# Attention in front of two Strassen layers on one core: loads three pairs ahead, four score blocks in a row, an immediate bias, tiles moved by 32 bytes

## The chip, the cores and the metric

The kernel runs on one core of one Trainium2 chip. The metric is the device time of one execution in microseconds (us); lower is better. Engines are called as the profile calls them: PE (TensorE, with PEld for its weight loads), DVE (VectorE), ACT (ScalarE), POOL (GpSimd), and SP, whose queue (SPq) issues nearly all DMAs.

## The reference, cut to what matters

```python
scores = scale * np.matmul(q, k.transpose(0, 1, 3, 2)) - np.log(S)   # 4 x 12 heads, S = 448, 64 wide
attn = 1.0 / (1.0 + np.exp(-scores))
out = np.matmul(attn, v)
x = out.transpose(0, 2, 1, 3).reshape(1792, 768)
h = x @ w_in;  x = (h * np.cos(h)) @ w_out                            # 768 -> 2048 -> 768
g = x @ w_gate                                                        # 768 -> 1536
y = (g / (1.0 + np.exp(-g)) * (x @ w_val)) @ w_out2                   # 1536 -> 768
```

Three stages follow each other: attention with a sigmoid in place of a softmax, layer 1 (cosine) and layer 2 (a gated pair). The weights arrive as float64.

## The kernel before

**Attention.** The 48 heads are taken as 24 pairs; two heads lie side by side in partitions 0 to 63 and 64 to 127. For a pair, `load` (L699) brings q and k into a slot of `raw_qk` (L704, two DMAs, three slots, `i % 3`), v into a tile `vs` (L706, three buffers), and the last 64 rows of v into a slot of `last_v` (L708, two small DMAs). `split` (L713) makes a high and a low part of q and k on DVE (tile `qk`, two buffers). `scores` (L720) computes one of four blocks: six matmuls into two of the six score banks, then one sigmoid on ACT (L731) from the banks into a tile `a`; its bias -log(448) is read from a one-column tile `nlog`. `weigh` (L734) multiplies the four blocks by v (L741) and ACT copies the result into the tile `r` (L743). In turn `i` of the pair loop the code issues: the loads of pair i+2, score blocks 0 to 2 of pair i, the split of pair i+1, `weigh(i - 1)`, and score block 3 of pair i. Every engine takes its instructions in the order in which the program lists them.

**Weight conversion.** Float64 weights are turned into float32 on the chip, one tile of 128x768 at a time: a DMA in (tile `lr` or `raw`), one ACT step, five DVE steps (or four and a second one on ACT), a DMA out to a scratch buffer (`swi`, `swo` and so on). Four lent sets of buffers do some of it beside attention (`lend_pool`), and the rest is done during layer 1. A converted tile comes back later into `t`, is summed (`sum`) and split (tiles `wa`, `wb`, `s`) for the matmuls.

**The two layers.** One level of Strassen: 28 units (16 in layer 1, 12 in layer 2) of seven products each (two times seven in layer 2; `seven`, L991, nine matmuls a product) and twelve down steps (`down`, L893, twelve matmuls a step). The moving operand is `x` for the products and `g` for the down steps. The seven combinations of x lie in two tiles: numbers 1, 5, 2 and 6 in `x0`, numbers 7, 3 and 4 in `x1`, which is opened on the other end of the memory when the lent buffers go.

**What sets the order.** An order written by a planner. `Order` simulates each engine with costs from the code; a task names an engine and a time, and the planner issues what can start first. During attention the planner is told by `beside` (L730, called at L767 and L772) how long a pair takes (5.75 us) and how much of each engine attention itself uses. Conversions fill what it believes to be free. So numbers in `beside` move instructions of all later stages too.

**Addresses.** Tiles of a pool lie one behind the other. The tile `small` (8 bytes a partition, 32 taken) stands ahead of `wa`, `s`, and of all that is opened after it on the same side: `qk`, `a`, `vs`, `wb`, `g`. All other sizes are multiples of 64 bytes; so these start 32 bytes behind a multiple of 64. `x0` lies ahead of `small`, on a multiple of 64 (and of 128). `x1` is laid from the other end and starts 96 bytes behind a multiple of 128.

Of the kernel before, what the change touches and what calls it, by code (L numbers as in the profile page):

```python
# [9 lines left out]
F32 = mybir.dt.float32  # L10
# [4 lines left out]
AF = mybir.ActivationFunctionType  # L15
# [135 lines left out]
def block_kernel(  # L151
# [53 lines left out]
    small = xp.tile([P, 2], F32, tag="small", name="small")  # L205
    nlog, warm = small[:, :1], small[:, 1:]
# [30 lines left out]
    LANDING = 5.0  # L237
    ENDS = ((17, 21),)
# [110 lines left out]
    def stashed(n):  # L349
        return False  # L350
# [153 lines left out]
    def operands():  # L504
# [34 lines left out]
        def stash_of(keys):  # L539
            n = keys[0][1] if keys[0][0] == "d" else keys[0][0]  # L540
            layer, h, c = units[n]
            return h, stashed(n), (layer, c) + keys[0][2 if keys[0][0] == "d" else 1:]
# [88 lines left out]
    def beside(time, span, **loads):  # L631

        for engine, load in loads.items():
            order.busy[engine] = max(order.busy.get(engine, 0.0), time) + load
        order.run(time + span)
# [51 lines left out]
    def attention():  # L687
        with tc.tile_pool(name="at", bufs=2) as at:
# [6 lines left out]
            zero = at.tile([P, S], mybir.dt.bfloat16, tag="z", name="z", bufs=1)  # L695
            raw_qk = at.tile([P, 3, 2, S], F32, tag="rqk", name="rqk", bufs=1)
            last_v = at.tile([P, 4, 2, D], F32, tag="lv", name="lv", bufs=1)

            def load(i, q_eng):  # L699

                raw = raw_qk[:, i % 3]
                vs = at.tile([P, NV], F32, tag="vs", name=f"vs{i}", bufs=3)
                for j, half in enumerate(heads):
                    q_eng[j].dma_start(out=raw[half], in_=qk[divmod(i, NP)][:, :, j])  # L704
                there = v[divmod(i, NP)]
                nc.sync.dma_start(out=vs, in_=there[:, :NV])  # L706
# [4 lines left out]
                qkv[i] = (raw, vs.rearrange("p (c j d) -> p c j d", j=2, d=D))  # L711
# [8 lines left out]
            def scores(i, c):  # L720
                both = parts[i]
                a = at.tile([P, 2, S], F32, tag="a", name=f"a{i}_{c}", bufs=8)
# [8 lines left out]
                nc.scalar.activation(out=a, in_=sc, func=AF.Sigmoid, bias=nlog, scale=1.0 / math.sqrt(D))  # L731
                prob[i, c] = a

            def weigh(i):  # L734
                _, vw = qkv.pop(i)
                o = banks[:, 6 + i % 2, :S]
                for c in range(NCH + 1):
                    a = prob.pop((i, c))
                    for j, half in enumerate(heads):
                        value = vw[:, c, j] if c < NCH else last_v[:, i % 4, j]  # L740
                        nc.tensor.matmul(o[half], lhsT=value, rhs=a[:, j], start=c == 0, stop=c == NCH)  # L741
# [14 lines left out]
            stops = []  # L756
            stops.append(lend_pool())
# [21 lines left out]
            time = 5.75 * NPAIR + 6.0  # L779
            beside(time, 3.8, ACT=0.6)  # L780
# [258 lines left out]
    with tc.manual_schedule():  # L1039
        nc.gpsimd.memset(nlog, -math.log(S))  # L1040
# [72 lines left out]
```

## Time and profile before

| | us |
|---|---|
| median of 3 runs (lowest to highest) | 1108.76 (1106.96 to 1112.98) |
| the profiled execution, its own time | 1111.78 |
| its span, first to last instruction | 1110.0 |
| attention, first score matmul to first matmul of layer 1 | 6.33 to 165.18 |
| layers 1 and 2 | 165.18 to 1110.0 |

The span is that of the profiled execution, and 1.78 us of its time lie around it. PE is busy for 97% of the span, but a busy PE need not be at its peak: the time is read from the spacing of its instructions and from the gaps ahead of them.

### The profile page before, as it was taken

The numbers are of one execution on the slowest core, as the hardware profiler recorded it, in microseconds if no ns is written. First come the engines' busy times: TensorE is split into PE (matmuls) and PEld (weight loads), VectorE is DVE, ScalarE is ACT, GpSimd is POOL, SyncE is SP. The second block draws the span as 40 slices with busy tenths as digits, with TensorE's granted clock in tenths as the row PEclk, the third lists the DMA queues.
The fourth block names the chain that finished last, engine by engine and source line by source line (L and its number), as shares of the span: only waits on it lengthen the run. The fifth ranks groups of instructions, "written<-read, shape, count | busy, mean of one in ns | idle before, by whom it ended". The sixth has DMA issues, their size and how long they took to land.

```text
span 1110.0 us, 14774 instructions
## 1 busy us (share of the span) xinstructions
PE 1079.7 (97%) x5507; PEld 931.4 (84%) x5507; DVE 843.9 (76%) x1135; ACT 668.7 (60%) x1001; POOL 130.2 (12%) x104
## 2 busy tenths in 40 slices
PE   7989999999999999999995999999999999999998
PEld 3544558999999899999995999999999999999997
DVE  3878968898899998888999898876459644555644
ACT  5778778777777787777786555544245344333330
POOL 0000000111022110111121200212111200110100
PEclk9999999999999999999998999999999999999999
DMA  8898635544544146455523565542121322112002
GB/s 238 277 249 247 177 110 191 204 168 162 185 149 137 57 149 221 143 179 190 195 91 115 184 225 203 212 142 86 44 71 58 126 88 71 46 55 72 29 1 100
DMA packets 64968, 156.69 MB, mean 141 GB/s; under 512 B 10624, under 2 KB 37248, under 8 KB 64896
## 3 DMA queue, kind: packets, MB, share of 16 engines
q1 hardware_dynamic: 64752, 155.51, 43.4%
q8 instruction: 43, 0.70, 0.3%
q10 hardware_dynamic: 144, 0.23, 0.1%
q14 instruction: 29, 0.24, 0.1%
HBM read 123.47 MB, written 32.24 MB: 140 GB/s over the span
## 4 chain that ended last, share of the span: by engine, by line
PE 83%; DVE 7%; DMA 6%; issue 1%; ACT 1%; SPq 1%; DVEq 0%; ACTq 0%
PE banks L991 43%; PE banks L893 34%; DMA rqk<-in_qk 6%; PE banks L741 3%; PE banks L727 2%; DVE r L229 2%; DVE x L229 1%; DVE u L229 1%; DVE qk L717 1%; DVE u L807 1%; SPq L704 1%; ACT a L731 0%; DVE g L229 0%; DVE qk L716 0%; DVE wa L229 0%
## 5 line engine op out<-in xcount | busy, mean ns | idle before, releaser
L893 PE MATMUL banks<-g,wb 128*128 128x448 f32 x1044 | 229.4, 368 | 0.3 <-DVE g L229 0.2
L991 PE MATMUL banks<-x,wb 128*128 128x448 f32 x1044 | 226.2, 365 | 0.0
L893 PEld LDWEIGHTS banks<-g,wb 128*128 128x128 f32 x1044 | 196.2, 188 | 18.6 <-DVE g L229 0.5
L991 PEld LDWEIGHTS banks<-x,wb 128*128 128x128 f32 x1044 | 196.1, 188 | 15.5 <-ACT banks L226 0.3
L893 PE MATMUL banks<-g,wa 128*128 128x448 f32 x720 | 161.3, 371 | 12.8 <-ACT g L226 11.4
L991 PE MATMUL banks<-x,wa 128*128 128x448 f32 x738 | 161.3, 365 | 0.0
L893 PEld LDWEIGHTS banks<-g,wa 128*128 128x128 f32 x720 | 136.8, 190 | 26.0 <-ACT g L226 11.8
L991 PEld LDWEIGHTS banks<-x,wa 128*128 128x128 f32 x738 | 138.6, 188 | 11.7 <-issue 0.7
L226 ACT ACTIVATE u<-u 128x448 f32<-128x448 f32 x175 | 97.6, 572 | 38.0 <-DVE u L229 27.8
L229 DVE TENSOR_TENSOR u<-u,banks 128x448 f32<-128x448 f32 x120 | 73.9, 617 | 60.8 <-PE banks L991 54.7
L229 DVE TENSOR_TENSOR r<-banks,r 128x896 f32<-128x896 f32 (+1 forms) x69 | 74.2, 1076 | 58.1 <-PE banks L893 57.6
L731 ACT ACTIVATE a<-banks,small 128x896 f32<-128x896 f32 x96 | 89.4, 1010 | 18.3 <-PE banks L727 18.3
L226 ACT ACTIVATE wb<-t 128x768 fp32r<-128x768 f32 x77 | 64.5, 840 | 42.8 <-PE banks L991 33.5
L229 DVE TENSOR_TENSOR wb<-t,wb 128x768 fp32r<-128x768 f32 x77 | 74.2, 967 | 20.5 <-ACT wb L226 20.0
L727 PEld LDWEIGHTS banks<-qk 64*128 64x128 f32 x576 | 50.6, 186 | 41.7 <-ACT a L731 11.4
L727 PE MATMUL banks<-qk 64*128 64x448 f32 x576 | 72.5, 384 | 12.0 <-DVE qk L716 5.7
L991 PE MATMUL banks<-x,s 128*128 128x448 f32 x360 | 80.0, 366 | 0.0
L226 ACT ACTIVATE g<-u 128x448 fp32r<-128x448 f32 x98 | 55.8, 572 | 34.8 <-PE banks L893 17.2
L226 ACT ACTIVATE r<-banks 128x896 f32<-128x896 f32 x52 | 47.8, 919 | 44.8 <-PE banks L893 44.7
L991 PEld LDWEIGHTS banks<-x,s 128*128 128x128 f32 x360 | 67.7, 188 | 5.9
L229 DVE TENSOR_TENSOR g<-u,g 128x448 fp32r<-128x448 f32 x98 | 64.8, 663 | 8.3 <-ACT g L226 8.2
L226 ACT ACTIVATE banks<-banks 128x448 f32<-128x448 f32 x80 | 42.3, 528 | 46.5 <-PE banks L991 45.0
(102 smaller groups left out, 1437.2 us busy)
## 6 DMA issues: line engine op xcount, KB each, us to landing
raw<-in_w_out SPq DMA_DIRECT2D x22, 768.0 KB, 5.5
t<-swi SPq DMA_DIRECT2D x32, 384.0 KB, 3.8
t<-swo SPq DMA_DIRECT2D x64, 192.0 KB, 2.9
rqk<-in_qk SPq DMA_DIRECT2D x47, 224.0 KB, 6.0
raw<-in_w_gate SPq DMA_DIRECT2D x12, 768.0 KB, 4.7
raw<-in_w_val SPq DMA_DIRECT2D x12, 768.0 KB, 4.9
lr<-in_w_in SPq DMA_DIRECT2D x9, 768.0 KB, 8.2
t<-swg SPq DMA_DIRECT2D x17, 384.0 KB, 3.2
```

Of the source, the lines that this page charges most:

```text
L226: return {"ACT": time}, lambda _: nc.scalar.activation(**kw)
L229: return {"DVE": time}, lambda _: nc.vector.tensor_tensor(out=out, in0=in0, in1=in1, op=op)
L704: q_eng[j].dma_start(out=raw[half], in_=qk[divmod(i, NP)][:, :, j])
L717: nc.vector.tensor_tensor(out=both[:, 1], in0=raw, in1=f32(both[:, 0]), op=SUB)
L727: nc.tensor.matmul(sc[:, j], lhsT=both[half, m, 1, starts[c]:starts[c] + P], rhs=both[half, p, 0], start=n == 0, stop=n == 2,)
L731: nc.scalar.activation(out=a, in_=sc, func=AF.Sigmoid, bias=nlog, scale=1.0 / math.sqrt(D))
L741: nc.tensor.matmul(o[half], lhsT=value, rhs=a[:, j], start=c == 0, stop=c == NCH)
L807: yield {"DVE": 0.62}, lambda _: nc.vector.scalar_tensor_tensor(out=u, in0=f, scalar=MAGIC, in1=u, op0=ALU.subtract, op1=ALU.subtract), ti ...
L893: nc.tensor.matmul(banks[:, first + e - d, :N], lhsT=w[:, m, e % KH, :], rhs=g[:, p], start=(i, m, p) == (0, 0, 0) and is_fresh and not pr ...
L991: nc.tensor.matmul(bank, lhsT=w[:, m, k, :], rhs=x[:, k, p, :], start=(k, m, p) == (0, 0, 0) and i in (1, 5), stop=(k, m) == (KH - 1, 1), ...
```

## The change

- The loads of q, k and v are issued three pairs ahead: four slots in `raw_qk`, five buffers of `vs`. `last_v` moves into the third part of `ring`, one slot for each pair of a batch, and is loaded for three pairs with two DMAs (`load_last`).
- The four score blocks of a pair stand in a row, and `weigh(i - 1)` behind them. `a` has seven buffers for eight.
- The bias of the sigmoid is an immediate number; the tile `small` goes, and a tile of 64 bytes (`warm`) takes its place, so that all tiles behind it move from 32 bytes behind a multiple of 64 to a multiple of 64. `x1` does not move. `zero` lies in `sums`.
- The planner's numbers for attention are new: 5.8 us a pair, and a load of each engine with a begin.

```diff
-    small = xp.tile([P, 2], F32, tag="small", name="small")
-    nlog, warm = small[:, :1], small[:, 1:]
+    warm = xp.tile([P, 16], F32, tag="warm", name="warm")
...
-        for engine, load in loads.items():
-            order.busy[engine] = max(order.busy.get(engine, 0.0), time) + load
+        for engine, (begin, load) in loads.items():
+            order.busy[engine] = max(order.busy.get(engine, 0.0), time + begin) + load
         order.run(time + span)
...
-            zero = at.tile([P, S], mybir.dt.bfloat16, tag="z", name="z", bufs=1)
-            raw_qk = at.tile([P, 3, 2, S], F32, tag="rqk", name="rqk", bufs=1)
-            last_v = at.tile([P, 4, 2, D], F32, tag="lv", name="lv", bufs=1)
+            zero = sums.bitcast(mybir.dt.bfloat16)[:, :S]
+            raw_qk = at.tile([P, 4, 2, S], F32, tag="rqk", name="rqk", bufs=1)
+            last_v = ring[:, 2].rearrange("p (s j d) -> p s j d", j=2, d=D)
+            NL = NP // 2
...
-                raw = raw_qk[:, i % 3]
-                vs = at.tile([P, NV], F32, tag="vs", name=f"vs{i}", bufs=3)
+                raw = raw_qk[:, i % 4]
+                vs = at.tile([P, NV], F32, tag="vs", name=f"vs{i}", bufs=5)
...
+            def load_last(i):
+
+                b, k = divmod(i, NP)
                 for j, half in enumerate(heads):
+                    there = v[b][k:k + NL, half, NV + P + j * D:NV + P + (j + 1) * D]
                     nc.sync.dma_start(
-                        out=last_v[heads[1], i % 4, j], in_=there[half, NV + P + j * D:NV + P + (j + 1) * D]
+                        out=last_v[heads[1], i % NP:i % NP + NL, j], in_=there.rearrange("s p d -> p s d")
                     )
...
-                a = at.tile([P, 2, S], F32, tag="a", name=f"a{i}_{c}", bufs=8)
+                a = at.tile([P, 2, S], F32, tag="a", name=f"a{i}_{c}", bufs=7)
...
-                nc.scalar.activation(out=a, in_=sc, func=AF.Sigmoid, bias=nlog, scale=1.0 / math.sqrt(D))
+                nc.scalar.activation(out=a, in_=sc, func=AF.Sigmoid, bias=-math.log(S), scale=1.0 / math.sqrt(D))
...
             load(1, (nc.sync, nc.sync))
+            load(2, (nc.sync, nc.sync))
+            load_last(0)
...
             for i in range(NPAIR):
-                if i + 2 < NPAIR:
-                    load(i + 2, (nc.sync, nc.sync))
-                time = 5.75 * i + 6.0
-                for c in range(NCH):
+                if i + 3 < NPAIR:
+                    load(i + 3, (nc.sync, nc.sync))
+                if i % NL == 1 and i + NL - 1 < NPAIR:
+                    load_last(i + NL - 1)
+                time = PAIR * i + 6.0
+                for c in range(NCH + 1):
                     scores(i, c)
+                parts.pop(i)
                 if i + 1 < NPAIR:
                     split(i + 1)
-                beside(time, 4.6, ACT=3.0, DVE=1.8, SP=3.0)
+                beside(time, 5.2, ACT=(0.85, 3.7), DVE=(0.0, 1.75), SP=(0.0, 2.0))
                 if i > 0:
                     weigh(i - 1)
-                scores(i, NCH)
-                parts.pop(i)
-                beside(time + 4.6, 1.15, ACT=1.6)
+                beside(time + 5.2, PAIR - 5.2, ACT=(0.3, 0.55))
```

**On SP, in attention.** The rows below are what SP has listed from the loads of pair 7 to those of pair 8 in the program before (`rqk` is `raw_qk`, `lt` and `lr` are buffers of the conversions, `lv` is `last_v`).

```order
L704 DMA rqk_80<-in_qk 64x2x448 x2
L706 DMA vs7_400<-in_v 128x384
L708 DMA lv_81<-in_v 64x64 x2
L235 DMA swi2_380<-lt2_119 128x768
L235 DMA swi3_434<-lt3_121 128x768
L235 DMA lr2_118<-in_w_in 128x1536
L235 DMA lr3_120<-in_w_in 128x1536
L704 DMA rqk_80<-in_qk 64x2x448 x2
L706 DMA vs8_461<-in_v 128x384
L708 DMA lv_81<-in_v 64x64 x2
```

And in the changed program, from the loads of pair 7 to those of pair 9.

```order
L705 DMA rqk_79<-in_qk 64x2x448 x2
L706 DMA vs7_329<-in_v 128x384
L714 DMA t_67<-in_v 64x3x64 x2
L234 DMA swi1_318<-lt1_117 128x768
L234 DMA t_67<-swi0_261 128x768
L234 DMA lr1_116<-in_w_out 128x1536
L705 DMA rqk_79<-in_qk 64x2x448 x2
L706 DMA vs8_389<-in_v 128x384
L234 DMA swi2_378<-lt2_119 128x768
L234 DMA t_67<-swi1_318 128x768
L234 DMA lr2_118<-in_w_in 128x1536
L705 DMA rqk_79<-in_qk 64x2x448 x2
```

A single conversion now stands between two pairs' loads, the small DMAs of `last_v` come every third pair (into `t`, which is `ring`), and in the whole of attention 13 conversions are listed for 15 before.

**On DVE, where layer 2 begins.** These are the last rows before, ahead of the row `g1_1492` for which PE's next down step waits; between the last row `r1_65<-banks_63,r1_65` above them and that row, 25 instructions are listed.

```order
L229 TENSOR_TENSOR wa0_70<-t_67,wa0_70 128x768
L807 SCALAR_TENSOR_TENSOR u4_1499<-u5_1500,u4_1499 128x448
L229 TENSOR_TENSOR g2_1493<-u3_1498,g2_1493 128x448
L229 TENSOR_TENSOR u0_1495<-u0_1495,banks_63 128x448
L436 TENSOR_SCALAR cv_1487<-cv_1487 128x768
L807 SCALAR_TENSOR_TENSOR u1_1496<-u5_1500,u1_1496 128x448
L439 SCALAR_TENSOR_TENSOR cv_1487<-raw0_1485,cv_1487 128x768
L229 TENSOR_TENSOR u4_1499<-u4_1499,banks_63 128x448
L229 TENSOR_TENSOR u1_1496<-u1_1496,u2_1497 128x448
L229 ISA cv_1487<-raw0_1485,cv_1487 128x1536
L510 TENSOR_TENSOR sum_68<-t_67 128x384
L229 TENSOR_TENSOR g1_1492<-u1_1496,g1_1492 128x448
```

In the changed program the row for the same down step is `g1_1440`, and these stand ahead of it.

```order
L814 SCALAR_TENSOR_TENSOR u2_1445<-u5_1448,u2_1445 128x448
L228 TENSOR_TENSOR x1_1325<-t3_1449,x1_1325 128x768
L228 TENSOR_TENSOR wb2_1438<-t_67,wb2_1438 128x768
L814 SCALAR_TENSOR_TENSOR u3_1446<-u5_1448,u3_1446 128x448
L228 TENSOR_TENSOR wa0_70<-t_67,wa0_70 128x768
L228 TENSOR_TENSOR u2_1445<-u2_1445,banks_63 128x448
L228 TENSOR_TENSOR x1_1325<-r0_64,x1_1325 128x3x448
L814 SCALAR_TENSOR_TENSOR u4_1447<-u5_1448,u4_1447 128x448
L228 TENSOR_TENSOR u3_1446<-u3_1446,u1_1444 128x448
L228 TENSOR_TENSOR g0_1439<-u2_1445,g0_1439 128x448
L228 TENSOR_TENSOR u4_1447<-u4_1447,u0_1443 128x448
L228 TENSOR_TENSOR g1_1440<-u3_1446,g1_1440 128x448
```

Ahead of these twelve rows, behind the corresponding row `r1_65<-banks_63,r1_65`, come three more (`x1_1325<-r0_64,x1_1325` twice and `r0_64<-r0_64`), so 14 instructions stand between; the conversion steps (`cv`) have moved behind `g1`.

**On DVE, where the second half of layer 1 begins.** Before, from the row `u1_1496<-u1_1496,banks_63` to the row `g0_1491`, whose end PE's down step needs:

```order
L229 TENSOR_TENSOR u1_1496<-u1_1496,banks_63 128x448
L229 TENSOR_TENSOR u4_1499<-u4_1499,u3_1498 128x448
L229 TENSOR_TENSOR g3_1494<-u0_1495,g3_1494 128x448
L229 TENSOR_TENSOR x1_1377<-r1_65,x1_1377 128x3x448
L229 TENSOR_TENSOR g0_1491<-u4_1499,g0_1491 128x448
```

In the changed program, from the corresponding `u3_1446` to `g1_1440`, which the same down step needs:

```order
L228 TENSOR_TENSOR u3_1446<-u3_1446,banks_63 128x448
L228 TENSOR_TENSOR x1_1325<-r1_65,x1_1325 128x3x448
L814 SCALAR_TENSOR_TENSOR u1_1444<-u5_1448,u1_1444 128x448
L228 TENSOR_TENSOR u2_1445<-u2_1445,u0_1443 128x448
L228 TENSOR_TENSOR x1_1325<-t_67,x1_1325 128x768
L228 TENSOR_TENSOR u1_1444<-u1_1444,u4_1447 128x448
L228 TENSOR_TENSOR g2_1441<-u2_1445,g2_1441 128x448
L228 TENSOR_TENSOR wb2_1438<-t3_1449,wb2_1438 128x768
L228 TENSOR_TENSOR g1_1440<-u1_1444,g1_1440 128x448
```

Three instructions stood between the first and the last row, and seven stand there now.

## Rows read from the trace of the kernel before

**Rows 1.** The page: busy time of each engine, share of the span, instructions.
```profile
PE 1079.7 (97%) x5507; PEld 931.4 (84%) x5507; DVE 843.9 (76%) x1135; ACT 668.7 (60%) x1001; POOL 130.2 (12%) x104
```

**Rows 2.** Busy time by stretch: length, engines, granted clock, DMA share, GB/s.
```profile
0.00:165.00 165.00, 151.80 (x971) 77.81 (x971) 119.21 (x146) 121.41 (x144) 3.82 (x8) 0.99 0.76 218
50.00:80.00 30.00, 26.77 (x168) 13.46 (x166) 22.02 (x31) 22.22 (x28) 0.31 (x1) 0.94 0.94 271
165.00:596.00 431.00, 429.34 (x2105) 395.05 (x2104) 388.72 (x535) 323.29 (x512) 66.65 (x48) 1.00 0.47 157
596.00:614.00 18.00, 6.25 (x20) 4.94 (x19) 16.24 (x25) 13.27 (x23) 4.96 (x2) 0.62 0.57 197
```

**Rows 3.** Timeline of PE: first scores, first weigh, a period, the stage's end.
```profile
6.33 0.47 PE L727 MATMUL banks<-qk 64*128 64x448 f32 x2 [0.88 <-DVE qk L716]
...
12.72 2.48 PE L741 MATMUL banks<-a,vs 128*64 128x448 f32 x12
...
125.19 2.92 PE L727 MATMUL banks<-qk 64*128 64x448 f32 x24
...
128.03 2.48 PE L741 MATMUL banks<-a,vs 128*64 128x448 f32 x12
...
131.19 2.09 PE L727 MATMUL banks<-qk 64*128 64x448 f32 x18
...
165.18 2.10 PE L991 MATMUL banks<-x,wa 128*128 128x448 f32 x9
```

**Rows 4.** Waits from 0 to 165 us: total, times, longest.
```profile
DVE qk L716 <- DMA rqk<-in_qk: 32.0, 13, 8.8
...
PEld banks L727 <- ACT a L731: 11.4, 20, 2.7
```

**Rows 5.** Waits of SP's own queue in the same stretch.
```profile
SPq L706 <- PE banks L741: 30.4, 18, 4.4
```

**Rows 6.** Line L704, the loads of q and k.
```profile
DMA to landing us min/median/max: 3.3/6.0/13.3
```

**Rows 7.** Timeline: the load of pair 8, and the DVE cast that needs it.
```profile
49.78 1.65 SPq L704 DMA_DIRECT2D rqk<-in_qk  x2
...
60.70 0.63 DVE L716 CAST qk<-rqk 128x896 fp32r<-128x896 f32 x1 [4.30 <-DMA rqk<-in_qk]
```

**Rows 8.** The page, groups of ACT: the sigmoid, and a copy of equal shape.
```profile
L731 ACT ACTIVATE a<-banks,small 128x896 f32<-128x896 f32 x96 | 89.4, 1010 | 18.3 <-PE banks L727 18.3
...
L226 ACT ACTIVATE r<-banks 128x896 f32<-128x896 f32 x52 | 47.8, 919 | 44.8 <-PE banks L893 44.7
```

**Rows 9.** Timeline of DVE and PE where layer 2 begins.
```profile
587.59 1.07 DVE L229 TENSOR_TENSOR r<-banks,r 128x896 f32<-128x896 f32 x1
...
589.98 4.48 DVE L229 TENSOR_TENSOR x<-r,x 128x1344 fp32r<-128x1344 f32 x3
...
600.60 0.95 DVE L229 TENSOR_TENSOR wb<-t,wb 128x768 fp32r<-128x768 f32 x1
...
608.31 0.74 PE L893 MATMUL banks<-g,wa 128*128 128x448 f32 x1 [11.38 <-ACT g L226]
...
608.75 0.62 DVE L229 TENSOR_TENSOR g<-u,g 128x448 fp32r<-128x448 f32 x1
```

**Rows 10.** Timeline of DVE where the second half of layer 1 begins.
```profile
372.91 0.61 DVE L229 TENSOR_TENSOR u<-u,banks 128x448 f32<-128x448 f32 x1
...
375.98 0.62 DVE L229 TENSOR_TENSOR g<-u,g 128x448 fp32r<-128x448 f32 x1
```

**Rows 11.** Timeline of PE: product 4, a down step, products 1 and 5.
```profile
561.28 1.96 PE L991 MATMUL banks<-x,wb 128*128 128x448 f32 x9
563.08 2.64 PE L893 MATMUL banks<-g,wb 128*128 128x448 f32 x12
565.56 2.00 PE L991 MATMUL banks<-x,wa 128*128 128x448 f32 x9
567.40 2.00 PE L991 MATMUL banks<-x,s 128*128 128x448 f32 x9
```

More of the change, by code (lines that the diff above doesn't have):

```diff
@@ L237, in block_kernel @@
     LANDING = 5.0
+    PAIR = 5.8
     ENDS = ((17, 21),)
@@ L541, in stash_of @@
             layer, h, c = units[n]
-            return h, stashed(n), (layer, c) + keys[0][2 if keys[0][0] == "d" else 1:]
+            return h, stashed(n), (layer, c) + (keys[0][2:] if keys[0][0] != "d" else ("d", *keys[0][2:]))
         def again(keys, size):
@@ L694, in attention @@
             chunk = itertools.count()
-            zero = at.tile([P, S], mybir.dt.bfloat16, tag="z", name="z", bufs=1)
-            raw_qk = at.tile([P, 3, 2, S], F32, tag="rqk", name="rqk", bufs=1)
-            last_v = at.tile([P, 4, 2, D], F32, tag="lv", name="lv", bufs=1)
+            zero = sums.bitcast(mybir.dt.bfloat16)[:, :S]
+            raw_qk = at.tile([P, 4, 2, S], F32, tag="rqk", name="rqk", bufs=1)
+            last_v = ring[:, 2].rearrange("p (s j d) -> p s j d", j=2, d=D)
+            NL = NP // 2
             def load(i, q_eng):
-                raw = raw_qk[:, i % 3]
-                vs = at.tile([P, NV], F32, tag="vs", name=f"vs{i}", bufs=3)
+                raw = raw_qk[:, i % 4]
+                vs = at.tile([P, NV], F32, tag="vs", name=f"vs{i}", bufs=5)
                 for j, half in enumerate(heads):
                     q_eng[j].dma_start(out=raw[half], in_=qk[divmod(i, NP)][:, :, j])
-                there = v[divmod(i, NP)]
-                nc.sync.dma_start(out=vs, in_=there[:, :NV])
+                nc.sync.dma_start(out=vs, in_=v[divmod(i, NP)][:, :NV])
+                qkv[i] = (raw, vs.rearrange("p (c j d) -> p c j d", j=2, d=D))
+            def load_last(i):
+                b, k = divmod(i, NP)
                 for j, half in enumerate(heads):
+                    there = v[b][k:k + NL, half, NV + P + j * D:NV + P + (j + 1) * D]
                     nc.sync.dma_start(
-                        out=last_v[heads[1], i % 4, j], in_=there[half, NV + P + j * D:NV + P + (j + 1) * D]
+                        out=last_v[heads[1], i % NP:i % NP + NL, j], in_=there.rearrange("s p d -> p s d")
                     )
-                qkv[i] = (raw, vs.rearrange("p (c j d) -> p c j d", j=2, d=D))
             def split(i):
@@ L739, in weigh @@
                     for j, half in enumerate(heads):
-                        value = vw[:, c, j] if c < NCH else last_v[:, i % 4, j]
+                        value = vw[:, c, j] if c < NCH else last_v[:, i % NP, j]
                         nc.tensor.matmul(o[half], lhsT=value, rhs=a[:, j], start=c == 0, stop=c == NCH)
@@ L748, in attention @@
             load(0, (nc.sync, nc.scalar))
-            nc.scalar.activation(out=warm, in_=nlog, func=AF.Sigmoid)
+            nc.scalar.activation(out=warm, in_=warm, func=AF.Sigmoid)
             nc.vector.memset(last_v[heads[0]], 0.0)
             load(1, (nc.sync, nc.sync))
+            load(2, (nc.sync, nc.sync))
+            load_last(0)
             for _ in range(11):
@@ L778, in attention @@
             weigh(NPAIR - 1)
-            time = 5.75 * NPAIR + 6.0
-            beside(time, 3.8, ACT=0.6)
+            time = PAIR * NPAIR + 6.0
+            beside(time, 3.8, ACT=(3.2, 0.55))
             order.now = time + 3.8
@@ L1039, in block_kernel @@
     with tc.manual_schedule():
-        nc.gpsimd.memset(nlog, -math.log(S))
+        nc.gpsimd.memset(warm, 0.0)
         for s in range(n_stages):
```

3 lines of the change are left out of this document (1 added, 2 removed).

## The prediction

> **What bounds the kernel now.** I read the page first: PE is busy for 97% of the span [rows 1]. That says only that PE is the engine to follow, since a late operand lengthens a stage without making PE look idle for long. So I cut the span into its stages [rows 2]. In attention, the first 165 us, PE has 151.80 us of busy time, so some 13 us are gaps; from 165 to 596 it is busy for 429.34 of 431 us, and nothing is to be had there except a shorter matmul; the stretch from 596 to 614, where layer 2 begins, has 6.25 us of PE in 18, at a granted clock of 0.62.
>
> The timeline of PE gives the period of attention when nothing is late [rows 3]: a run of 24 score matmuls begins at 125.19, the twelve matmuls of `weigh` at 128.03, the next run at 131.19. That is 2.84 + 3.16 = 6.0 us a pair. From the first `weigh`, at 12.72, to the end of attention, at 165.18, are 152.5 us; 24 periods are 144.
>
> What was late is in the list of waits [rows 4]: `split`'s cast on DVE waited 32.0 us, 13 times, for the q and k of the next pair. SP's own queue says why [rows 5]: the load of v (L706) waited 30.4 us, 18 times, for a matmul of `weigh` (L741). `vs` has three buffers, so the load of v for pair i+2 needs the buffer of pair i-1, whose `weigh` stands later in the same turn. SP takes its work in order, so the transfers listed behind it, and then the next pair's q and k, go out late too. Such a load takes 3.3 to 13.3 us to land [rows 6]. One instance in full [rows 7]: pair 8's load is issued at 49.78, the cast that needs it runs at 60.70, 10.9 us later, and its engine had waited 4.30 us.
>
> **The change part by part: loads.** With five buffers of `vs` and four slots of `raw_qk`, the load for pair i+3 needs `weigh(i - 2)` and `split(i - 1)`, both of the turn before; SP need not stand still for them. The rows of the changed order show one conversion between two pairs' loads, and small DMAs only every third pair. A pair is loaded three periods, 18 us, ahead of its scores; the split before them, whose first step takes 0.63 us [rows 7], needs 2 us at most, an estimate. That leaves 16 us, more than the longest landing of 13.3 us.
>
> **Four blocks in a row.** Before, block 3 of a pair and blocks 0 to 2 of the next already made one run of 24 score matmuls on PE. The change shifts by one block, 2.92 / 4 = 0.73 us, which pair stands in the run: the period stays 6.0 us, the first `weigh` moves to 12.72 + 0.73 = 13.45, `weigh(22)` to 13.45 + 22 x 6.0 = 145.45, and the last follows it directly. Attention ends without waits at 145.45 + 2 x 3.16 = 151.8, that is 165.18 - 151.8 = **13.4 us earlier**. The split is wanted one block earlier; the earlier loads cover that, and without their cover it costs 0.73 us in each of the 13 turns that waited, 9.5 us. All of the 13.4 will not come: the first pairs' loads still share the channel with conversions, whose share of DMA is 0.94 from 50 to 80 us [rows 2]. I leave a fifth of it as waits, **+2.7**; the bounds are 0 and all 13.4.
>
> **The bias.** A sigmoid with its bias read from a tile takes 1010 ns; ACT's copy of the same shape, from the same memory and with numbers in the instruction, takes 919 ns [rows 8]. I take the difference, 0.09 us, for each sigmoid: a different function is compared, so the bounds are 0 and 0.09. It matters only where PE waits for ACT, which it did 20 times in attention for 11.4 us [rows 4], at the fourth block of a run, which needs the banks that the first block's sigmoid has read. I take 0.09 for each of 22 steady pairs, **-2.0**.
>
> **`a` with seven buffers.** Block 3 of a pair takes the buffer of block 0 of the pair before, free once the first quarter of `weigh` has read it. ACT reaches it about then, after three sigmoids. I put 0; if ACT waits there, up to a quarter of `weigh` (0.8 us) in each turn, 18 us in all, is the upper bound, but it would have to come on top of ACT's slack: 121.41 of 165 us busy [rows 2]. `zero`, `warm` and the fewer small DMAs are off the path: 0.
>
> **Where layer 2 begins.** PE waits 11.38 us ahead of a down step at 608.31, which ends when `g1` is ready (608.75 for its last row); the profile names ACT, but DVE is what ran without a pause from 587.59 [rows 9]. Between the row `r1` at 587.59 and `g1`, 25 instructions stood, 21.2 us. Now 14 stand there. Of those, four are 1344 wide (4.48 / 3 = 1.49 us each), three are 768 wide (0.95) and seven 448 wide (0.62), and `r1` itself is 1.07 [rows 9]: 5.96 + 2.85 + 4.34 + 1.07 = 14.2 us, 7.0 earlier; 0.7 more if their spacing is a little below their durations, as it is for the row of three. I take -7.3. While PE stood idle its clock fell: at 0.2 us a matmul its 20 instructions would be 4.1 us, and they took 6.25 [rows 2], some 2 us more. With a gap of 4 us part of that comes back: -1.2. Together **-8.5**; bounds 0, if DVE reaches `r1` later by as much, and -11.4 - 1 - 2 = -14.
>
> **Second half of layer 1.** From 372.91 to 375.98 DVE needs 3.07 us with three instructions between [rows 10]. By their durations those and the first are 0.61 + 2 x 0.62 + 1.49 = 3.3, so the spacing is 0.92 of the durations. Now seven stand there, four of 448 columns, two of 768 and one of 1344: 0.61 + 4 x 0.62 + 2 x 0.95 + 1.49 = 6.5, at 0.92 of it 6.0 us. PE waits for the end: **+2.9**; bounds 0 (if DVE arrives early) and 5 (if its own wait comes on top).
>
> **Addresses.** The timeline shows what the matmuls cost by their moving tile [rows 11]. From start to start, product 4 (moving `x1`, which does not move) takes (563.08 - 561.28) / 9 = 0.200 us, the down step (moving `g`, 32 bytes behind a multiple of 64) (565.56 - 563.08) / 12 = 0.207, product 1 (moving `x0`, on a multiple of 128) (567.40 - 565.56) / 9 = 0.204. `x0` is aligned already and no faster than `x1`, which lies 96 behind a multiple of 128: so being aligned is not what makes a matmul fast here. Down steps have 28 x 12 x 6 = 2016 matmuls with `g`, four products in seven move `x0`: 1440 matmuls, three `x1`: 1080. If the move brought all to 0.200, 2016 x 6.7 ns + 1440 x 4.4 ns = 20 us would go. If what makes `x1` fast is its place relative to its weights, which now move, 1080 x 6.7 ns = 7 us would come. Of -20 and +7 I take **0**, nearest to the row of `x0`, which is where the moved tiles will stand. The Trainium skill (SBUF — State Buffer, Specifications) gives SBUF a cacheline of 16 bytes, two hits on which give full bandwidth. By that rule a shift of 32 bytes changes nothing and the sum has 0 here; the rows with 0.200 and 0.207 for matmuls of equal form say that something other than it is at work.
>
> **The sum.** -13.4 + 2.7 - 2.0 - 8.5 + 2.9 = -18.3 us against the profiled 1111.78. The median of the runs is 3.0 below that execution, so 1108.76 - 18.3 = **1090 us**. Elsewhere the new numbers of the planner shift conversions: 13 instead of 15 in attention, so two more of some 3.6 us of DVE in layer 1, where DVE is busy for 388.72 of 431 us [rows 2]. They fit in the 42 us left; without that cover they would cost 7 us.
>
> **The rivals.**
> Alignment helps: half of the 20 us bound comes, 1090 - 10 = 1080 us. For it speaks that 2016 matmuls of the down steps are the slowest and all are moved; against it the row of `x0`.
> The channel is the limit: where DMA has a share of 0.94, loads issued earlier only stand in line longer. Half of the 10.7 comes, and a faster sigmoid then hides behind late loads: -5.4 - 8.5 + 2.9 = -11.0, 1098 us. For it speaks the 13.3 us landing; against it the 30.4 us in which SP stood still with work to issue.
> The layers keep their waits: DVE, with two more conversions, arrives at layer 2 later by what it saves there. Then -13.4 + 2.7 - 2.0 + 2.9 = -9.8, 1099 us.
> Slower: ACT's conversion step stands in order between the sigmoids and `weigh`'s copy. With loads three pairs ahead in the queues, the conversion's own tile `lr` may land after ACT comes to it; ACT then holds up the next sigmoid and PE behind it. 13 such steps stand in attention: at 18.3 / 13 = 1.4 us each the gain is gone, at 1.83 us each the kernel is 0.5% slower (1114 us). Against it: the order lists the load of each such tile one turn or more ahead of its step.
> The change does little: PE's waits for DMA are traded one for one for waits for ACT, and DVE keeps its delay, 1105 to 1108 us.
>
> **Chances.** 0.5% of 1108.76 is 5.5 us, about what a measurement of this kernel can tell from no change. The forecast, 0.56 (by itself 1084 to 1096); alignment helps, 0.14; the channel, 0.14; the layers keep their waits, 0.10; little changes, 0.03; slower, 0.03. The range 1078 to 1101 holds the forecast, both partial cases and the nearer half of the alignment case; left out are its farther half, 0.07, the last two cases, 0.06, and mishaps that add up, about 0.07. The first four lie below 1103.2 save for 0.03 of their ends: faster 0.91, same 0.06, slower 0.03.
>
> **What would show it.** In attention: SP's wait for `weigh` gone; DVE's wait for q and k below 5 us; a `weigh` every 6.0 us; the first matmul of layer 1 at 152 to 156. A sigmoid near 920 ns. Ahead of the down step where layer 2 begins a gap near 4 us; in the second half of layer 1 one of some 3 us. The spacing of the down steps still 0.207 and of product 4 0.200. Wrong would make it: a spacing that moves by over 2 ns on thousands of matmuls, an ACT row that waits for `lr`, or DVE's waits moving to `rqk` again.

## The result, and the profile after

The changed kernel takes 1099.62 us (5 runs, 1096.12 to 1102.72) against 1108.76 for the kernel before: a ratio of 0.9914, interval 0.9891 to 0.9937, 9.1 us faster. The forecast was 1090, with 1078 to 1101 as its range: the sign and the range hold, the size is half of what was forecast. The profiled execution spans 1097.8 us, 12.2 less than that of before.

The stretches of PE (columns as in [rows 2]):

```profile
0.00:151.20 151.20, 148.06 (x971) 78.71 (x972) 114.36 (x136) 113.19 (x141) 5.11 (x9) 1.00 0.80 222
151.20:580.00 428.80, 423.39 (x2063) 388.21 (x2062) 389.32 (x540) 322.62 (x510) 56.12 (x41) 1.00 0.47 157
360.00:372.00 12.00, 8.78 (x35) 7.44 (x34) 11.37 (x16) 8.79 (x17) 1.93 (x1) 0.86 0.33 100
589.00:601.00 12.00, 6.75 (x19) 5.36 (x18) 10.18 (x16) 7.86 (x16) 8.92 (x3) 0.72 0.67 246
```

Attention has 148.06 us of PE in 151.20, 3 us of gaps where 13 us were; the layers, though, take from 151.20 to 1097.8, 946.6 us, where they took 944.8. Two stretches stand out in them, both at a lowered granted clock (0.86 and 0.72). So between these two traces the change won 14.0 us in attention and lost 1.8 behind it.

**Attention.** Its timeline on PE, at its end:

```profile
136.37 2.82 PE L732 MATMUL banks<-qk 64*128 64x448 f32 x24
...
142.27 2.83 PE L732 MATMUL banks<-qk 64*128 64x448 f32 x24
145.04 2.48 PE L746 MATMUL banks<-a,vs 128*64 128x448 f32 x12
...
148.09 2.43 PE L746 MATMUL banks<-a,vs 128*64 128x448 f32 x12
...
151.20 2.09 PE L998 MATMUL banks<-x,wa 128*128 128x448 f32 x9
```

The period is 142.27 - 136.37 = 5.90 us, for 6.0 before [rows 3]. `weigh(22)` begins at 145.04, forecast 145.45, and nothing stands between it and the last `weigh`. The waits up to 160 us, and those of SP's queue (the columns of [rows 4] and [rows 5]):

```profile
DVE qk L721 <- DMA rqk<-in_qk: 12.4, 5, 4.8
...
ACT a L736 <- PE banks L746: 7.5, 23, 0.3
PEld banks L732 <- ACT a L736: 6.9, 25, 1.2
```
```profile
SPq L706 <- PE banks L746: 15.3, 8, 4.2
```

DVE's wait for q and k fell from 32.0 to 12.4 us, and what is left of it hardly reaches PE, whose own waits for DVE are, before and after:

```profile
PE banks L727 <- DVE qk L716: 5.7, 4, 2.7
PE banks L727 <- DVE qk L717: 3.0, 6, 0.7
```
```profile
PE banks L732 <- DVE qk L721: 0.8, 1, 0.8
```

Two signs that the prediction had named did not come: SP's wait for `weigh` is not gone, and DVE's is not below 5 us. SP still waits 15.3 us, but now ahead of need, so that it costs nothing here: the effect on the consumer tells a harmful wait of a queue from a harmless one. ACT waits 23 times for `weigh`'s first quarter, which is the seventh buffer of `a`; at 0.3 us at most it shows in no longer period. The sigmoid is as short as was forecast (columns of [rows 8]):

```profile
L736 ACT ACTIVATE a<-banks 128x896 f32<-128x896 f32 x96 | 82.9, 920 | 19.5 <-PE banks L732 12.0
```

**The layers.** The gaps on PE, and DVE ahead of the one where layer 2 begins:

```profile
339.15 0.48 PE L900 MATMUL banks<-g,wa 128*128 128x448 f32 x1 [0.45 <-ACT g L225]
340.48 3.15 PE L900 MATMUL banks<-g,wa 128*128 128x448 f32 x14 [0.85 <-DVE g L228]
...
366.15 0.47 PE L900 MATMUL banks<-g,wa 128*128 128x448 f32 x1 [2.36 <-ACT g L225]
367.48 3.50 PE L900 MATMUL banks<-g,wa 128*128 128x448 f32 x11 [0.86 <-DVE g L228]
...
594.69 5.25 PE L900 MATMUL banks<-g,wa 128*128 128x448 f32 x12 [5.22 <-ACT g L225]
```
```profile
580.17 1.08 DVE L228 TENSOR_TENSOR r<-banks,r 128x896 f32<-128x896 f32 x1
...
593.39 0.61 DVE L228 TENSOR_TENSOR g<-u,g 128x448 fp32r<-128x448 f32 x1
593.92 0.95 DVE L228 CUSTOM_DVE_ANT_0 t<-raw,t 128x1536 uint16<-128x1536 uint16 x1
594.79 0.61 DVE L228 TENSOR_TENSOR g<-u,g 128x448 fp32r<-128x448 f32 x1
```

The gap at layer 2 shrank from 11.38 to 5.22 us. `g1` came at 593.39, 13.2 us behind `r1` (forecast: 13.5 to 14.2). But the first down step there moves `g2` in the changed program, and that came 1.4 us later still. Behind the gap 12 matmuls take 5.25 us, ten of them at 0.37 us from start to start: PE's clock was at the lower of its two levels, 1.2 of 2.4 GHz (0.50 in the rows below, first before, then after).

```profile
599.60:613.20 13.60, 4.52 (x11) 3.69 (x12) 12.64 (x21) 9.37 (x18) 4.16 (x2) 0.50 0.63 224
```
```profile
593.90:600.70 6.80, 5.98 (x15) 4.98 (x16) 5.23 (x8) 3.35 (x7) 6.64 (x3) 0.50 0.75 269
```

The low clock lasted half as long as before, 6.8 us for 13.6. But before it had begun 8.7 us ahead of PE's first matmul (608.31) and was spent mostly on idle time; now it begins 0.8 us ahead of it, and more matmuls fall into it, 13 for 9. At 366 the gaps grew by 2.4 us, near the forecast 2.9, but they too have matmuls at the low clock behind them (eight at 0.37 us), and the gap at 340 was not forecast.

**The matmuls.** For every matmul of the layers I took the time from its start to the next start from the records, left out those over 230 ns (22 to 48 in each kernel), and took means by the tile moved and by the tile with the weights of the next matmul, since these are loaded meanwhile. Behind each tile stands where it starts, modulo 128 bytes ("low" are `wa`, `wb`, `s`; "tail" are the weights that lie in the last part of `x1`'s tile):

| ns, mean | before | changed |
|---|---|---|
| `g`, weights low | 205.2 (32, 32) | 204.3 (64, 64) |
| `x0`, weights low | 204.3 (0, 32) | 202.1 (0, 64) |
| `x1`, weights low | 200.4 (96, 32) | 205.6 (96, 64) |
| `g`, weights in the tail | 201.9 (32, 96) | 203.7 (64, 96) |

`x1`, which did not move, lost 5 ns a matmul; `x0`, which did not move either, won 2. 920 x 5.1 + 261 x 1.7 - 1228 x 2.2 - 1737 x 0.9 ns = +0.9 us: the addresses matter, and the change spent as much as it won. The intervals left out exceed 204 ns by 17.6 us in all before and by 18.4 us now, +0.8; the two together are nearly the 1.8 us that the layers lost.

### The profile page after: what moved, and what is told of

It reads as the page before. It is cut to its first block, busy times and chain, and to the rows that moved or that the text cites. A ratio compares the mean times of both kernels' runs of the same rounds, so it can differ in the third digit from the quotient of the medians.

```text
span 1097.8 us, 14763 instructions
## 1 busy us (share of the span) xinstructions
PE 1080.3 (98%) x5507; PEld 933.7 (85%) x5507; DVE 849.6 (77%) x1139; ACT 663.5 (60%) x1002; POOL 126.4 (12%) x99
## 4 chain that ended last, share of the span: by engine, by line
PE 89%; DVE 8%; ACT 1%; issue 1%; DMA 0%; DVEq 0%; ACTq 0%
PE banks L998 42%; PE banks L900 34%; PE banks L746 7%; PE banks L732 6%; DVE r L228 2%; DVE x L228 2%; DVE u L228 1%; DVE g L228 1%; DVE wb L228 1%; DVE u L814 1%; DMA rqk<-in_qk 0%; DVE wa L228 0%; ACT u L225 0%; DVE t L433 0%; DVE x L658 0%
## 5 line engine op out<-in xcount | busy, mean ns | idle before, releaser
L998 PE MATMUL banks<-x,wb 128*128 128x448 f32 x1044 | 228.9, 367 | 0.0
L900 PEld LDWEIGHTS banks<-g,wb 128*128 128x128 f32 x1044 | 196.0, 188 | 18.3 <-DVE g L228 1.1
L225 ACT ACTIVATE u<-u 128x448 f32<-128x448 f32 x179 | 99.8, 571 | 44.2 <-DVE u L228 26.8
L736 ACT ACTIVATE a<-banks 128x896 f32<-128x896 f32 x96 | 82.9, 920 | 19.5 <-PE banks L732 12.0
L228 DVE TENSOR_TENSOR wb<-t,wb 128x768 fp32r<-128x768 f32 x73 | 69.3, 955 | 14.0 <-ACT wb L225 13.4
L225 ACT ACTIVATE wb<-t 128x768 fp32r<-128x768 f32 x73 | 60.7, 837 | 25.3 <-PE banks L998 17.7
L510 POOL TENSOR_TENSOR sum<-t 128x384 f32<-128x384 f32 x20 | 34.1, 1704 | 333.8 <-DMA t<-swi 93.0
L732 PE MATMUL banks<-qk 64*128 64x448 f32 x576 | 69.8, 386 | 2.0 <-ACT a L736 0.8
```

The lines of the kernel that those rows point to most:

```text
L225: return {"ACT": time}, lambda _: nc.scalar.activation(**kw)
L228: return {"DVE": time}, lambda _: nc.vector.tensor_tensor(out=out, in0=in0, in1=in1, op=op)
L510: on.tensor_tensor(out=out, in0=a, in1=b, op=op)
L732: nc.tensor.matmul(sc[:, j], lhsT=both[half, m, 1, starts[c]:starts[c] + P], rhs=both[half, p, 0], start=n == 0, stop=n == 2,)
L736: nc.scalar.activation(out=a, in_=sc, func=AF.Sigmoid, bias=-math.log(S), scale=1.0 / math.sqrt(D))
L900: nc.tensor.matmul(banks[:, first + e - d, :N], lhsT=w[:, m, e % KH, :], rhs=g[:, p], start=(i, m, p) == (0, 0, 0) and is_fresh and not pr ...
```

## The experiments

**Which distance is fast.** In the table the groups at 200 to 202 ns have 64 bytes between the starts, modulo 128. Four kernels move one tile each, by a tile of padding that nothing uses: three lower `x1` (with the tail weights in it) by 96, 64 and 32 bytes, one lifts `g` (and the tiles behind it, which no matmul reads) by 64.

```diff
             x1 = xr.tile([P, 3 * size + 2 * WT], F32R, tag="x1", name="x1")
+            xr.tile([P, 24], F32, tag="pad", name="pad")     # x1_at_0; 16 in x1_at_32; 8 in x1_at_64
...
+            mp.tile([P, 16], F32, tag="pad", name="pad")     # g_at_0, alone
             for i in range(4):
                 gslots.give(mp.tile([P, 2, N], F32R, tag=f"g{i}", name=f"g{i}"))
```

> The changed kernel with x1 96 bytes lower, so that it starts on a multiple of 128; nothing else moves. Before, product matmuls that move x1 with weights in wa, wb or s took 200.4 ns from start to start (x1 96 behind a multiple of 128, weights 32 behind); in the changed kernel, with the weights at 64, they take 205.6. Theory of halves: a matmul is slow when its moving tile and the weights loaded meanwhile for the next one start in the same 64-byte half of 128 bytes. Then these 920 matmuls come back to 200 to 202 ns, about 4 us less in all; matmuls of x0 with weights kept in x1's tail go from 202.6 to about 204, those of g with such weights from 203.7 to about 202. Theory of alignment (a moving tile on a multiple of 64 is fast): also about 200 to 202, x0 and g unchanged. Theory of place (x1 lost speed through something else, such as the order of work): 205 to 206, nothing changes.

> The changed kernel with x1 64 bytes lower, 32 behind a multiple of 128, the weights at 64. Theory of halves: the other half, so x1's matmuls fall from 205.6 to 200 to 202 ns although x1 is not on a multiple of 64. Theory of alignment: 205 or slower. Theory of a distance of exactly 64 bytes between the two starts (which fits the two kernels as well): the distance is now 32, so 205 to 206.

> The changed kernel with x1 32 bytes lower, on a multiple of 64 like the weights (64 behind a multiple of 128 both). Theory of halves, and theory of a distance of 64: same half, so x1's matmuls stay at 205 to 206 ns. Theory of alignment: they fall to 200 to 202.

> The changed kernel with a tile of 64 bytes ahead of g, so that g starts on a multiple of 128 while all weights stay at 64. Theory of halves: the down steps' matmuls (1725 of them with weights in wa, wb, s) fall from 204.3 to 200 to 202 ns, 4 to 7 us less in all; x0 (202.1) and x1 (205.6) unchanged. Theory of alignment: nothing changes, g was on a multiple of 64 already. Rival that g's matmuls are slow since ACT or DVE write g and the banks beside them: nothing changes.

Measured, means of the same groups in ns:

| | changed | x1_at_0 | x1_at_32 | x1_at_64 | g_at_0 | apart |
|---|---|---|---|---|---|---|
| `x1` starts at | 96 | 0 | 32 | 64 | 96 | 0 |
| `x1`, weights low (64) | 205.6 | 201.9 | 204.1 | 206.5 | 206.1 | 202.5 |
| `g` starts at | 64 | 64 | 64 | 64 | 0 | 0 |
| `g`, weights low (64) | 204.3 | 205.5 | 205.9 | 206.1 | 200.3 | 200.6 |
| tail weights start at | 96 | 0 | 32 | 64 | 96 | 64 |
| `g`, weights in the tail | 203.7 | 201.8 | 206.0 | 206.6 | 204.8 | 200.4 |
| `x0` (0), weights low (64) | 202.1 | 202.1 | 202.2 | 202.0 | 202.3 | 202.3 |
| layers, first to last start, us | 942.7 | 941.6 | 943.7 | 946.2 | 935.7 | 931.9 |

The first four were run once each: 1097.06, 1106.21, 1102.15 and 1091.67 us. These times hold attention too, which ended between 149.8 and 156.8 us in them, so the means and the layers' row decide. The timeline of PE in g_at_0: down steps at (549.36 - 546.96) / 12 = 0.200 us a matmul, the product of `x1` between them at 1.86 / 9 = 0.207:

```profile
546.96 2.56 PE L900 MATMUL banks<-g,wb 128*128 128x448 f32 x12
549.36 2.02 PE L998 MATMUL banks<-x,wb 128*128 128x448 f32 x9
551.22 2.56 PE L900 MATMUL banks<-g,wb 128*128 128x448 f32 x12
```

and in x1_at_32, down steps at 0.207, the product at 1.84 / 9 = 0.204:

```profile
553.04 2.64 PE L901 MATMUL banks<-g,wb 128*128 128x448 f32 x12
555.52 2.00 PE L999 MATMUL banks<-x,wa 128*128 128x448 f32 x9
557.36 2.64 PE L901 MATMUL banks<-g,wb 128*128 128x448 f32 x12
```

The theory of alignment falls: `x1` at 64 is the slowest of its four places. The theory of halves, which I held first, falls too: `x1` at 32 is in the other half than its weights and comes only to 204.1 (over half of these matmuls at 205 or more), and `g` with tail weights is at 206.0 there (64 against 32). What all fast groups have in these tables is a distance of 64 between the two starts. In x1_at_0 `g` got slower by 1.3 ns without being moved, which none of the theories says; it took back 2.2 of the 3.3 us that `x1` won.

**All tiles apart.** The sum of these, with the weights behind `x1` moved to 64 as well:

```diff
-            x1 = xr.tile([P, 3 * size + 2 * WT], F32R, tag="x1", name="x1")
+            x1 = xr.tile([P, 3 * size + 16 + 2 * WT], F32R, tag="x1", name="x1")
+            xr.tile([P, 8], F32, tag="pad", name="pad")
...
-            pairs.give(x1[:, 3 * size:].rearrange("p (m a k c) -> p m a k c", m=2, a=2, k=KH))
+            pairs.give(x1[:, 3 * size + 16:].rearrange("p (m a k c) -> p m a k c", m=2, a=2, k=KH))
...
+            mp.tile([P, 16], F32, tag="pad", name="pad")     # ahead of g
```

> The changed kernel with every moving tile 64 bytes (of 128) away from the weights: g and x1 on multiples of 128, the weights that lie behind x1 moved to 64 like all others. Theory of a distance of 64: all groups of layer matmuls run at 200 to 202 ns. From the groups of the changed kernel: 1725 matmuls of g 204.3 to 200.3, 261 of g with weights behind x1 203.7 to 200.3, 920 of x1 205.6 to 201.9, 159 of x1 with such weights 204.3 to 202: some 6.9 + 0.9 + 3.4 + 0.4 = 11.6 us less, so 1088 us. Rival: what g gains comes back elsewhere (PE runs into later operands, since ACT and DVE do not get faster): gaps of PE grow, and less than half, under 6 us, is left.

It takes 1089.22 us, ratio to before 0.9820 (0.9786 to 0.9854): faster than both kernels, and 10.4 us faster than the changed one, where 11.6 were expected. The layers are 10.8 us shorter, and the rival falls: the intervals over 230 ns exceed 204 ns by 17.7 us in all, for 18.4 in the changed kernel. A product and a down step there take 1.83 / 9 = 0.203 and 2.41 / 12 = 0.201:

```profile
541.85 1.99 PE L999 MATMUL banks<-x,wb 128*128 128x448 f32 x9
543.68 2.57 PE L901 MATMUL banks<-g,wb 128*128 128x448 f32 x12
546.09 1.98 PE L999 MATMUL banks<-x,wa 128*128 128x448 f32 x9
```

The score matmuls move q and load k from one tile, at the same place modulo 128. The next kernel puts 64 bytes between them.

```diff
-                both = at.tile([P, 2, 2, S], F32R, tag="qk", name=f"qk{i}")
+                both = at.tile([P, 2, 2, S + 16], F32R, tag="qk", name=f"qk{i}")[:, :, :, :S]
```

> The kernel apart with q and k of a pair 64 bytes of 128 apart as well (64 bytes of padding between them; the score matmuls move q and load k). Theory of a distance of 64: a pair of concurrent score matmuls takes some 200 ns from pair to pair and would take 196, 24 x 12 x 4 ns = 1.2 us less in all. Rival: the scores are held by the banks, that is by ACT, and nothing changes; both are within what the comparison can tell, so the trace decides.

1090.88 us, 0.9832 (0.9795 to 0.9869): no difference from apart. From one pair of score matmuls to the next the mean, of times under 230 ns, is 204.5 ns in apart and 205.0 here, and the period of attention is 5.92 us. So no gain shows for two matmuls at a time on half the rows.

**The addresses back.** The change without its address part: a tile of 32 bytes in place of 64.

```diff
-    warm = xp.tile([P, 16], F32, tag="warm", name="warm")
+    warm = xp.tile([P, 8], F32, tag="warm", name="warm")
```

> The changed kernel with a tile of 32 bytes in place of the 64, so that qk, a, vs, wa, wb, s and g start 32 bytes behind a multiple of 64 again; all instructions are the same. Theory that only the distance of 64 between moving tile and weights is fast: x1 (96 against 32) 200 to 201 ns again, x0 (0 against 32) 204 to 205, g 205: 920 x 5.1 ns less, 1220 x 2.2 and 1725 x 0.9 ns more, some 0.5 us less in all: the address part of the change is worth nothing. Rival that multiples of 64 bytes help: 3 us or more slower.

`x1` 200.5 ns, `x0` 204.3, `g` 204.9; the layers take 941.7 us for 942.7, and the time is 1096.97 us, 0.9894 (0.9860 to 0.9927). As expected, the part is worth nothing that can be told, and if anything a microsecond of loss.

**The loads.** First all of the loads undone, then only the lead.

```diff
-            raw_qk = at.tile([P, 4, 2, S], F32, tag="rqk", name="rqk", bufs=1)
+            raw_qk = at.tile([P, 3, 2, S], F32, tag="rqk", name="rqk", bufs=1)     # loads_undone only
-                raw = raw_qk[:, i % 4]
-                vs = at.tile([P, NV], F32, tag="vs", name=f"vs{i}", bufs=5)
+                raw = raw_qk[:, i % 3]                                             # loads_undone only
+                vs = at.tile([P, NV], F32, tag="vs", name=f"vs{i}", bufs=3)        # loads_undone only
-            load(2, (nc.sync, nc.sync))
-                if i + 3 < NPAIR:
-                    load(i + 3, (nc.sync, nc.sync))
+                if i + 2 < NPAIR:                                                  # both
+                    load(i + 2, (nc.sync, nc.sync))
```

> The changed kernel with the loads as before: two pairs ahead, three slots of raw_qk, three buffers of vs; the loads of last_v, the order of the blocks, the bias, the addresses and the planner's numbers stay changed. Theory that the buffers and the lead made attention shorter: SP waits for weigh again, 20 us or more in all, and attention ends 8 to 14 us later than at 151.2: some 1108 to 1112 us. Rival that the planner's order (one conversion between two pairs' loads) did it: attention ends below 155, the time is up by under 4 us.

> The changed kernel with loads issued two pairs ahead but with its four slots and five buffers. If the buffers of vs were the cause (SP stood still for weigh), SP's wait for weigh is gone and attention ends at 151 to 154: 0 to 3 us more than the changed kernel. If the lead itself counts (landings up to 13.3 us against two periods of 5.9 us less 2 us for the split), DVE waits for q and k in several turns and attention ends at 156 to 160: 5 to 9 us more.

Without the loads the gain is gone: 1109.02 us, 1.0005 (0.9980 to 1.0031), 9.4 us above the changed kernel, and attention ends at 160.56. Its waits, up to 165 us:

```profile
SPq L706 <- PE banks L746: 57.7, 20, 7.5
```
```profile
DVE qk L721 <- DMA rqk<-in_qk: 37.6, 13, 8.9
```

With the buffers but two pairs of lead it is 1104.03, 0.9945 (0.9924 to 0.9965), and attention ends at 156.42:

```profile
DVE qk L721 <- DMA rqk<-in_qk: 22.2, 8, 8.6
```

So the buffers bring about half, 1109.02 to 1104.03; the intervals of the two kernels do not overlap. SP's wait for `weigh` at L706 fell to 1.2 us there, less than in the changed kernel, and attention is longer all the same. Whether the lead brings the rest the times alone can't tell, since the intervals of lead_two and of the changed kernel overlap, nor can DVE's wait, which is 12.4 us in the changed kernel but 19.0 in moved_back with the same loads. The turns can. From the first `weigh` to the tenth, lead_two and then the changed kernel:

```profile
13.91 2.48 PE L746 MATMUL banks<-a,vs 128*64 128x448 f32 x12
...
72.19 2.48 PE L746 MATMUL banks<-a,vs 128*64 128x448 f32 x12
```
```profile
13.99 2.48 PE L746 MATMUL banks<-a,vs 128*64 128x448 f32 x12
...
67.20 2.48 PE L746 MATMUL banks<-a,vs 128*64 128x448 f32 x12
```

58.3 us against 53.2, and in the six kernels whose attention differs from the changed one's in addresses alone (the four above, apart and moved_back) 53.2 to 53.8. So the lead brings the rest, some 5 us in its trace.

**The bias.** A tile for the bias again, at no new address.

```diff
-    warm = xp.tile([P, 16], F32, tag="warm", name="warm")
+    small = xp.tile([P, 16], F32, tag="warm", name="warm")
+    warm, nlog = small[:, :1], small[:, 1:2]
...
-                nc.scalar.activation(out=a, in_=sc, func=AF.Sigmoid, bias=-math.log(S), scale=1.0 / math.sqrt(D))
+                nc.scalar.activation(out=a, in_=sc, func=AF.Sigmoid, bias=nlog, scale=1.0 / math.sqrt(D))
...
+        nc.gpsimd.memset(nlog, -math.log(S))
```

> The changed kernel with the sigmoid's bias read from a one-column tile as before; no address moves. Theory: a sigmoid takes 1010 ns for 920, and PE waits for it once a pair: the period of attention goes from 5.91 to 6.00 us, 22 x 0.09 = 2 us more in all. Rival that the bias is hidden: the period stays 5.91, 0 us.

The sigmoid takes 1006 ns, and the period is 144.00 - 138.01 = 5.99 us, in nearly every turn:

```profile
138.01 2.91 PE L733 MATMUL banks<-qk 64*128 64x448 f32 x24
140.84 2.48 PE L747 MATMUL banks<-a,vs 128*64 128x448 f32 x12
...
144.00 2.91 PE L733 MATMUL banks<-qk 64*128 64x448 f32 x24
```

Attention ends at 153.01, 1.8 us later. The total, 1099.77 us and 0.9902 (0.9875 to 0.9928), can't tell 2 us; the period can.

**The order of the blocks.** Three blocks, split, `weigh`, and the fourth, as before.

```diff
-                for c in range(NCH + 1):
+                for c in range(NCH):
                     scores(i, c)
-                parts.pop(i)
...
                     weigh(i - 1)
+                scores(i, NCH)
+                parts.pop(i)
```

> The changed kernel with the order of turns as before: three score blocks, split, weigh, the fourth block; seven buffers of a, loads and all else as changed. Theory that a row of four only shifts which pair stands in a run: the period stays 5.9 us and the first weigh comes 0.7 us earlier; 0 to 1 us. Rival that with four in a row the split and ACT's steps come in better time: a longer period or new waits of the split, 3 us or more slower.

The period stays 5.92 us, as expected. The time is 1103.16 us, 0.9942 (0.9916 to 0.9968), 3.5 us above the changed kernel. Of these the trace shows 0.8 at the end, where the last fourth block now stands ahead of the last `weigh`:

```profile
151.63 0.87 PE L732 MATMUL banks<-qk 64*128 64x448 f32 x6
152.44 2.48 PE L746 MATMUL banks<-a,vs 128*64 128x448 f32 x12
```

The rest lies in two turns, 9.63 and 6.86 us long, around pairs 15 and 16. In the first of them an ACT step of the layers, listed ahead of the sigmoids, waits for DVE:

```profile
102.10 1.32 ACT L656 ACTIVATE x<-r 128x1344 fp32r<-128x1344 f32 x1 [4.01 <-DVE r L228]
```

In the second, `weigh`'s twelve matmuls take 3.40 us for 2.48, the first of them at the lower clock. But moved_back, which has the changed order, has 8.27 and 7.59 there, by the same step (the last section). Whether the row of four brings more than 0.8 us stays open.

**The planner's numbers.**

```diff
-    PAIR = 5.8
+    PAIR = 5.75
...
-                beside(time, 5.2, ACT=(0.85, 3.7), DVE=(0.0, 1.75), SP=(0.0, 2.0))
+                beside(time, 4.6, ACT=(0.0, 3.0), DVE=(0.0, 1.8), SP=(0.0, 3.0))
...
-                beside(time + 5.2, PAIR - 5.2, ACT=(0.3, 0.55))
+                beside(time + 4.6, 1.15, ACT=(0.0, 1.6))
...
-            beside(time, 3.8, ACT=(3.2, 0.55))
+            beside(time, 3.8, ACT=(0.0, 0.6))
```

> The changed kernel with the planner's numbers for attention as before (5.75 us a pair, the old loads of ACT, DVE and SP). The order on DVE is then that of the kernel before in nearly every row. Theory that the new numbers only move waits in the layers: the gap where layer 2 begins grows from 6.5 back to 11 to 13 us, the gaps near 363 and 338 us (3.2 and 1.3 us idle, and half clock behind the first) go, so the layers take what they took, 940 to 944 us; attention, with 15 conversions for 13, ends 0 to 4 us later: 1100 to 1104 us. Rival that the new numbers brought much of the gain: 1106 us or more.

The old gap is back, and the one at 366 is a third as long:

```profile
366.82 2.50 PE L900 MATMUL banks<-g,wa 128*128 128x448 f32 x11 [1.07 <-DVE g L228]
...
598.36 0.74 PE L900 MATMUL banks<-g,wa 128*128 128x448 f32 x1 [11.43 <-ACT g L225]
```

Yet the layers take 942.8 us from the first start to the last, against 942.7. The new numbers took 6 us of waiting from one place of the layers and gave it to two others. The time is 1102.67 us, 0.9935 (0.9911 to 0.9959), as was expected, though its interval overlaps that of the changed kernel. Attention, with its 15 conversions, ends at 155.28; from the first `weigh` to the tenth it takes 55.5 us for 53.2, so in its trace some 2 us of the gain in attention came with the new numbers.

## Why the prediction was half right

- **Loads, waits and bias:** forecast -13.4 + 2.7 - 2.0 = -12.7, in the traces 165.18 - 151.20 = -14.0. The mechanism is shown by loads_undone and lead_two, the 0.09 us of the bias by bias_tile. Fewer waits were left in this trace than I had set aside. The step that SP need not stand still for `weigh` did not hold, but its waits no longer reached PE.
- **Where layer 2 begins:** forecast -8.5. This is the term that failed. The gaps there, over the usual spacing, went from 12.8 to 6.3 us, 6.5 less for my 7.3, since I took `g1` for the row that PE needs and the changed program needs `g2`, 1.4 us behind it. And of the clock I took back 1.2 us for a shorter gap, while 13 matmuls instead of 9 ran at the low level, 0.7 us more: the low stretch was half as long, but it lay on the matmuls and no longer on the gap. In all -5.8.
- **Second half of layer 1:** forecast +2.9 for the wait alone; the gaps grew by 2.4, and with the eight matmuls at the low clock behind them it was +3.9. The gap at 340 (+1.8) I had not looked for: I followed the two places where the order of DVE had changed most, and not each `g` that PE waits for.
- So the three places give -5.8 + 3.9 + 1.8 = -0.1 for the forecast -5.6, and plan_old shows that they belong together. The **rival** in which the layers keep their waits (1099 us, chance 0.10) is what happened, not by DVE arriving later but by waits at other places.
- **Addresses:** forecast 0, +0.9 measured, but not for my reason, and so by luck: some 5 us lost with `x1` and `g` in front of tail weights stood against 4 won with the rest. A spacing that moves by over 2 ns on thousands of matmuls was my own sign of being wrong, and it came. I took the row of `x0` for the place where moved tiles would stand; `x0` itself became faster as its weights moved, and `x1` slower. The bound that I had named, that `x1`'s speed hangs on its place relative to its weights, was the mechanism, and about half of the -20 us bound comes with another placement: apart is 10.4 us faster than the changed kernel. The Trainium skill gives SBUF lines of 16 bytes (SBUF — State Buffer, Specifications). That a shift of 32 bytes changes nothing, which I took from it, does not hold here: `x1`'s matmuls went from 200.4 to 205.6 ns by such a shift of their weights.
- **The base:** the sum, -18.3, stood against the profiled execution; the traces differ by 12.2 and the medians by 9.1. The profiled execution of before lay 3.0 above its median, that of the changed kernel on its median. That those 3 us were waits in attention, which the change removes only once, is likely but only argued: over the kernels whose attention differs from the changed one's in addresses alone, its end lies between 149.8 and 156.8 us.

## What to carry to other kernels

When a queue stands still for a buffer, count the buffers first and the lead second, and see who is late behind the queue. Changed numbers of a planner move waits in every later stage: list each place where the bound engine waits, before and after, and sum them all, each with the matmuls at the low clock behind it. Where matmuls of equal form differ by a few ns, compare where the moved tile and the weights start modulo 128 bytes, before moving either.

## What was not expected of the hardware

Full matmuls (128 x 128 weights, 448 columns) took 200.3 to 202.5 ns from start to start where the moved tile and the next weights start 64 bytes apart modulo 128, and 204.1 to 206.5 at the other distances tried (0, 32 and 96), with weights in the low tiles. Small groups with weights in the tail do not all fit: `x0` took 202.6 at a distance of 32, and `x1`, whose tail weights are always at a distance of 0 but in apart, took 202.3 to 206.5 according to its place. `g` in x1_at_0 slowed without being moved. So a distance of 64 was fast wherever it was tried with full matmuls, and why the others differ among themselves is open.

The one wait left in attention is ACT's, for a step of the layers listed ahead of `weigh`'s copy and the next sigmoids. In the changed kernel, ACT, then PE, and last ACT in moved_back:

```profile
100.22 1.33 ACT L656 ACTIVATE x<-r 128x1344 fp32r<-128x1344 f32 x1 [1.47 <-DVE r L228]
```
```profile
102.83 0.88 PE L732 MATMUL banks<-qk 64*128 64x448 f32 x6 [0.84 <-ACT a L736]
```
```profile
103.11 1.32 ACT L656 ACTIVATE x<-r 128x1344 fp32r<-128x1344 f32 x1 [2.86 <-DVE r L228]
```

In moved_back PE waited 2.17 us for it, and the twelve matmuls of `weigh` behind it ran at the lower clock, 4.17 us for 2.48; in g_at_0 no turn is longer than 5.92 us. This step, and the clock behind it, make most of the spread between the kernels in which attention differs in addresses alone. It resembles the slower rival, an ACT step that holds up the sigmoids, but it is a single step of the layers that waits for DVE, and none of the thirteen conversions that wait for `lr`.
